# V rows of every second head from pair 12 on loaded from ScalarE's queue, with a new order of the work

## The chip, the cores and the metric

The kernel runs on one core of one Trainium2 chip. Its time is the device time of the execution in microseconds (us), and the time of a version is the median of several runs. The engines are called as in the profile: PE (TensorE; PEld are its weight loads), ACT (ScalarE), DVE (VectorE), POOL (GpSimd) and SP (SyncE, which only issues DMAs). SP and ACT each have a hardware DMA queue, POOL a software one.

## The reference

Attention over 8 batches with 8 heads of 576 positions and 64 features, in two parts that are added, followed by a two-layer network over the 4608 tokens:

```
q_d, k_d, v_d = means over groups of 4 positions            # 144 positions
out_up    = repeat(softmax(scale * q_d k_d^T) v_d, 4)        # pooled attention
out_local = softmax(scale * q k^T where |i - j| < 4) v       # a band of 7 positions
x = (out_up + out_local) as 4608 tokens x 512 features
h = x @ w_in                                                 # 512 -> 2048
result = (h - tanh(h)) @ w_out                               # 2048 -> 512
```

## The kernel before

The work comes in 32 *pairs* of heads (pair p is batch p // 4, heads 2(p % 4) and the next) and 8 *blocks* of the network, one for each batch. Four pairs make the tokens of one block. Matmuls run in bf16.

**A pair** (`attention`, `prep_v`, `pool_v`, `pool_v4`). `load_qk` brings K and Q rows into `st` (4 slots, p % 4), `load_v` brings the V rows of each of the two heads by a DMA of its own into `vst` (5 slots, p % 5; L390, 160 KB, 640 rows of 256 bytes). From pair 12 on, `load_v4` also brings V in groups of four positions (`v4`), which POOL adds up (L440, L444); the first 12 pairs pool V by matmuls (L458). Casts to bf16 follow (`qr` L502, `vw` L427), then transposes of K and Q: on PE for the first 12 pairs (L510), by DMA from SP afterwards (L556). Scores are matmuls over 64 rows (L657, L665, L671), followed on ACT by three exps (L676, L680, L684), by a mask product (L711) on DVE or POOL, by the matmuls with V (L725), by the division (L740, L742) and the way back into token columns `xT` (L767 on PE or L780 by DMA, L760).

**A block** (`dense`). 16 groups of four matmuls of 512 columns against `w_in` (L803), each followed by a tanh on ACT (L814) and a subtraction on DVE (L817, `gT`); and the second layer (L883, for the last three blocks L1030), whose results are copied out and stored. The 64 tokens of a batch beyond 512 are done for two batches at once (L829, L855). The groups of both layers take four PSUM banks in turn (`DENSE`). `w_in` and `w_out` come by four DMAs each from POOL (`load_w`, L408 and L412), held back until a tile named by `GATE` or `OGATE` has arrived (L416).

**The order.** Everything is written down as operations for a planner (`Plan`): `op` notes an operation with the engine, a cost in ns, what it reads and writes, a priority and a time before which it isn't started (`after`). `order` puts all operations on a time line greedily: of what is ready it takes, on each engine, the one with the lowest priority number, and it frees a buffer when its readers are done. `emit` then writes the program in the order of the planned starts, so the planner decides what stands behind what on each engine's queue. Where several engines can do an operation, the string `GIVEN` names one by a letter for each choice; `REL` gives the release time of each pair's casts, `ONE` the pairs whose scores are issued together, `SOFT` the pairs whose `v4` loads come from POOL. A load (`load`) is two planned operations: the issue, on the engine that is named (500 ns on SP), and the transfer, on one planned DMA resource.

**What is not in the plan.** In the built program the DMAs of both hardware queues take eight completion semaphores in turn (DMAHW0 to DMAHW7), in the order of the program and whichever engine issues them. Each issue waits until the DMA that used its semaphore before, which is the one eight places earlier, has landed. The planner knows nothing of these waits. Each engine works its instructions off in order, so what stands behind a waiting issue waits too.

Of the kernel before, what the change touches and what calls it, by code (L numbers as in the profile page):

```python
# [14 lines left out]
class Plan:  # L15
# [17 lines left out]
    def op(self, eng, ns, fn, reads=(), writes=(), pri=0, after=0.0, slack=0.0,  # L33
           port=False, opens=None, uses=(), choice=None, rows=128, share=0.4):
        i = len(self.ops)
        deps = set()
        for key in reads:
            if key in self.last_write:
                deps.add(self.last_write[key])
        for key in writes:  # L40
            if key in self.last_write:
                deps.add(self.last_write[key])
            deps.update(self.readers.get(key, ()))
        for key in reads:
            self.readers.setdefault(key, set()).add(i)
        for key in writes:
            self.last_write[key] = i
            self.readers[key] = set()
        deps.discard(i)
        names = set(uses)  # L50
        if opens and not isinstance(opens, list):
            opens = [opens]
        for o in opens or ():
            names.add(o[0])
        for n in names:
            self.users.setdefault(n, []).append(i)
        if choice:

            letter = self.given[self.choices]
            self.choices += 1  # L60
            named = [a[:4] for a in choice if a[0][0] == letter]
            choice = named or [a for a in choice if len(a) == 4]
        alts = {a[0]: a for a in choice} if choice else {eng: (eng, ns, fn, port)}
        self.ops.append(dict(alts=alts, deps=deps, pri=pri, after=after, slack=slack,
                             opens=opens, names=names, rows=rows, share=share,
                             what=(list(writes) + [None])[0]))
        return i
# [135 lines left out]
def kernel(  # L203
# [9 lines left out]
    nc = tc.nc  # L213
    B, H, S, D = q.shape
# [5 lines left out]
    SCALE = 1.0 / float(D) ** 0.5  # L220
    N_FF = Dff // 128
    N_DC = Dm // 128
    WIDE = [c == "1" for c in "1011"]
    NBLK, NR, LEFT = B, 3, S - 512
    STEP = 112
    NT = 5
# [12 lines left out]


    KIN = [c == "1" for c in "11111111111100000000000000000000"]
    HALF = [c == "1" for c in "00001000000000000000000000000000"]

    SOFT = [c == "1" for c in "00001110011000110010001001000001"]
    VIN = [c == "1" for c in "11111111111100000000000000000000"]
    BACK = [c == "1" for c in "11111111111100000000000000000000"]
    ONE = [c == "1" for c in "00000000010000001111111111111111"]
    REL = [
# [4 lines left out]
    ]  # L253

    GIVEN = (
        "..A..D.DADA.PADDADPDD.AADD..D.DD.AA.DA.ADAA....ADAD..AA..P...AP.D..AP....DDPPPDD"
        "..D..A.A...PAAAPPPAADDD.DDDDAD.ADAD.A..PPPDDDAA...A.....DA..A.AA.PD.D..ADPDDAP.P"
        "D.PP..D.DDDDD.P..DP...DADP...P....A...D.PP..DPAAPP..P.D..AD..A..DD.PPD.PA..D.P.."
        ".PPD.P........P..PDDD.PD...AAPD....D.PPDPD.A...DPPD..A.DP.DPPP....AD..DP.D.DAP.."
        "D....DPP..DAAD..DPP.D.AA.PD.PP.PPPAAPDD..P..D..DAPP.DPP.P.P.PPAA.PPP.PPPAA.D.PPP"  # L260
        "DPDP.P..DDDD.D."
    )

    const = ctx.enter_context(tc.tile_pool(name="const", bufs=1))
# [2 lines left out]
    def fixed(name, shape, dt, n=None, pool=const):  # L267
        if n is None:
            return pool.tile(shape, dt, name=name, tag=name)
        return [pool.tile(shape, dt, name=f"{name}{i}", tag=f"{name}{i}")  # L270
                for i in range(n)]
# [12 lines left out]
    st = fixed("st", [128, 2, 2, 4 * D], FP32, NST)  # L284
# [3 lines left out]
    vst = fixed("vst", [128, 2, NT, D], FP32, NVST)  # L288
# [28 lines left out]
    P = Plan(GIVEN)  # L317
# [40 lines left out]
    def load(ns, fn, keys, cost, pri, after=0.0, eng="SP"):  # L358
        op(eng, ns, fn, writes=list(keys) + [("q", keys[0])], pri=pri, after=after)
        op("DMA", cost, None, reads=[("q", keys[0])], writes=keys, pri=pri,  # L360
           share=0.18 if keys[0][0] == "vst" else 0.35)
# [22 lines left out]
    def load_v(p):  # L384
        b, j, s = p // NP, p % NP, p % NVST
        for i in range(2):
            base = v[b, 2 * j + i]

            def issue(i=i, base=base):
                nc.sync.dma_start(out=vst[s][:, i], in_=bass.AP(  # L390
                    tensor=base.tensor, offset=base.offset,
                    ap=[[D, 128], [STEP * D, NT], [1, D]]))
            load(500, issue, [("vst", s, i)], 940, 10 * p - 3000 + 5)

    def load_v4(p):
        b, h0, s = p // NP, 2 * (p % NP), p % NV4
        vv = v[b, h0:h0 + 2].rearrange("h (g c) d -> g h (c d)", c=4)
        for i in range(2):
            load(770 if SOFT[p] else 450,
                 lambda i=i: (nc.gpsimd if SOFT[p] else nc.sync).dma_start(  # L400
                     out=v4[s][0:128 - 112 * i, :, i], in_=vv[128 * i:144 - 16 * (1 - i)]),
                 [("v4", s, i)], 1000 - 870 * i, 10 * p - 3000 + 6,
                 eng="POOL" if SOFT[p] else "SP")

# [67 lines left out]
    def attention(p):  # L472
        b, j, s = p // NP, p % NP, p % 2
        sn, w, k3 = p % NST, p % NVW, p % NKQ
        early = KIN[p]
        split = HALF[p] and not early
        pri = 10 * p
# [183 lines left out]
        def score2():  # L661
            ps = at(s2)
            for hh in range(2):
                rows = slice(64 * hh, 64 * hh + 64)
                T.matmul(ps[:, hh, 0:120], kt[s][rows, STEP * 4:STEP * 4 + 128],  # L665
                         kq[k3][rows, :, 1, G0[4]:G0[4] + NG[4]],
                         start=True, stop=True)
            for i in range(2):
                for hh in range(2):
                    rows = slice(64 * hh, 64 * hh + 64)  # L670
                    T.matmul(ps[:, hh, 120 + G * i:120 + G * i + G],  # L671
                             qkd[s][rows, 128 * i:128 * i + 128],
                             qkd[s][rows, G + GAP:2 * G + GAP], start=True, stop=True)
# [15 lines left out]
        def both_scores():  # L689
            score1()  # L690
            score2()
        if not ONE[p]:
            op("PE", 220 * cold, score1, rows=64,
# [259 lines left out]
    def token_sums(kb, which):  # L953
        g = kb % 2
        a11, a12, a21, a22 = quarters(kb)
        for n, dst, x0, x1, sub, h in ((0, S0, a21, a22, 0, 2), (2, a21, a11, a21, 1, 0),
                                       (1, a11, S0, a11, 1, 0), (3, a12, a12, a11, 1, 1)):
            if n not in which:
                continue
            parts = [(0, 1)] if WIDE[n] else [(0,), (1,)]  # L960
            for es in parts:
# [182 lines left out]
        for _ in steps:  # L1144
            pass

    GATE, OGATE = ("st", 2, 0), ("vst", 1, 1)
    SEVEN = [c == "1" for c in "00000111"]
    ORDER7 = (1, 2, 6, 7, 4, 5, 3), (1, 7, 2, 6, 5, 4, 3)
    DENSE = [(7,), (6,), (5,), (4,)]  # L1150
# [37 lines left out]
    for p in range(NP):  # L1188
        if p + 1 < NP:
            load_qk(p + 1)  # L1190
        load_v(p)
# [4 lines left out]
    def load_next():  # L1196
        if nl[0] < NPAIR:
            if nl[0] % NP == 0:
                load_rest(nl[0] // NP)
            load_qk(nl[0])  # L1200
            load_v(nl[0])
            nl[0] += 1
        if nl[0] == NP + 4:
            for f in range(4):
                load_w(moe_w_out, w_out_sb, "w_out", f, OGATE if f == 0 else None)
# [66 lines left out]
```

## Time and profile before

| what | us |
|---|---|
| median of 3 runs | 324.42 |
| the runs | 323.06 to 325.06 |
| the profiled execution | 322.44 |
| its span on the core | 320.7 |
| PE busy | 309.1 |
| DVE busy | 255.3 |
| ACT busy | 207.8 |
| POOL busy | 156.8 |

A line of the timeline gives start, duration, engine, line, operation, the tile written and the tile read, and how many were merged (x4); engines with a q are their sequencers, which issue DMAs. The rows of digits cut the span into 40 slices of 8 us and give the busy share in tenths. A line of windows gives, for each engine, busy time and instructions in that stretch, then the granted clock of PE, the mean share of the 16 DMA engines (it goes above 1 where several queues are served at once) and GB/s. The line "DMA to landing" gives the time from issue to the last byte's landing.

### The profile page before, as it was taken

To read this page: it belongs to the slowest core of one execution; us is meant where nothing else is said; L and a number is where in the kernel's file an instruction comes from. 1 tells how busy PE (TensorE), PEld (TensorE's weight loads), DVE (VectorE), ACT (ScalarE), POOL (GpSimd) and SP (SyncE) were. 2 spreads that over 40 slices of the span, in tenths; PEclk is the share of its full clock that TensorE was granted. 3 is DMA by queue.
4 is the path that set the end of the run, shared out by engine and by line. 5 is a ranking of instruction groups with operands and counts; after the bars stand their busy time and mean duration, and the time that the engine had idled before them with its cause. 6 is when DMAs were issued, how large, how long until landed. Compare 5 with 4: busy or idle time off the path is not lost.

```text
span 320.7 us, 7553 instructions
## 1 busy us (share of the span) xinstructions
PE 309.1 (96%) x2831; PEld 181.0 (56%) x2831; DVE 255.3 (80%) x451; ACT 207.8 (65%) x372; POOL 156.8 (49%) x185
## 2 busy tenths in 40 slices
PE   7978999999999999999999999999899999999994
PEld 3654546554754545454655444545476667666783
DVE  5685997597888898679888999899999797656853
ACT  5884995588856776369745878579766852455210
POOL 7822664326267473537464735357794653511000
PEclk9999999999999999999999999999999999999999
DMA  8999999999999999999999999995452143200414
GB/s 218 275 219 227 279 185 247 289 277 304 240 232 274 236 210 246 224 255 195 245 222 177 269 237 251 232 223 112 94 92 57 35 49 93 67 0 3 130 36 131
DMA packets 117205, 59.23 MB, mean 185 GB/s; under 512 B 85008, under 2 KB 112592, under 8 KB 117168
## 3 DMA queue, kind: packets, MB, share of 16 engines
q1 hardware_dynamic: 111584, 52.17, 71.3%
q0 software_dynamic: 4896, 5.97, 10.0%
q10 hardware_dynamic: 688, 0.61, 0.6%
q8 instruction: 22, 0.36, 0.4%
q14 instruction: 15, 0.12, 0.1%
HBM read 43.65 MB, written 9.44 MB: 166 GB/s over the span
## 4 chain that ended last, share of the span: by engine, by line
PE 88%; DMA 7%; DVE 1%; SPq 1%; ACT 0%; POOL 0%; ACTq 0%; issue 0%; POOLq 0%
PE ps L803 34%; PE ps L883 22%; PE ps L1030 11%; DMA vst<-in_v_dram 6%; PE ps L725 5%; PE ps L829 5%; PE ps L855 4%; PE ps L657 3%; DMA sr<-in_q_dram 1%; PE ps L671 1%; PE ps L510 1%; PE ps L458 1%; PE ps L767 1%; PE ps L665 1%; SPq L366 1%; DVE xT L760 1%
## 5 line engine op out<-in xcount | busy, mean ns | idle before, releaser
L803 PE MATMUL ps<-xT,w_in_sb 128*128 128x512 bf16 x512 | 124.6, 379 | 0.0
L817 DVE TENSOR_TENSOR gT<-ps,u 128x512 bf16<-128x512 f32 x128 | 86.0, 684 | 21.2 <-ACT u L814 19.6
L814 ACT ACTIVATE u<-ps 128x512 f32<-128x512 f32 x128 | 76.1, 599 | 36.2 <-PE ps L803 33.6
L883 PE MATMUL ps<-w_out_sb,gT 128*128 128x512 bf16 x320 | 78.6, 379 | 0.0
L803 PEld LDWEIGHTS <-w_in_sb 128*128 128x128 bf16 x512 | 47.1, 98 | 47.3 <-issue 0.4
L883 PEld LDWEIGHTS <-gT 128*128 128x128 bf16 x320 | 29.2, 98 | 31.2
L444 POOL TENSOR_TENSOR vp<-v 128x256 bf16<-128x256 f32 x20 | 14.6, 730 | 58.7 <-PE ps L725 48.1
L676 ACT ACTIVATE E<-ps 128x912 bf16<-128x912 f32 x32 | 29.8, 931 | 17.8 <-PE ps L665 14.6
L1030 PEld LDWEIGHTS <-gT 128*128 128x128 bf16 x288 | 27.9, 98 | 7.5
L742 DVE TENSOR_TENSOR ln<-ps,r 128x768 bf16<-128x768 f32 x32 | 30.6, 956 | 0.9
L711 DVE TENSOR_TENSOR E<-E,mask 128x1152 bf16<-128x1152 bf16 x29 | 25.6, 882 | 4.4 <-ACT E L680 4.2
L502 POOL CAST qr<-st 128x512 bf16<-128x512 f32 x32 | 22.5, 713 | 9.3 <-DMA st<-in_q_dram 6.0
L440 POOL TENSOR_TENSOR v<-v 128x512 f32<-128x512 f32 x20 | 25.4, 1271 | 1.1
L725 PEld LDWEIGHTS <-E 128*128 128x128 bf16 x576 | 21.7, 97 | 6.1
L684 ACT ACTIVATE E<-ps 128x576 bf16<-128x576 f32 x32 | 20.9, 654 | 0.0
L583 ACT COPY kt<-kq 128x576 bf16<-128x576 bf16 x16 | 18.9, 1180 | 2.9 <-DVE kq L578 2.7
L593 POOL TENSOR_TENSOR half<-kq 128x576 f32<-128x576 bf16 x13 | 18.1, 1389 | 3.6 <-DVE kq L578 1.5
L725 PE MATMUL ps<-vw,E 128*128 128x65 bf16 x320 | 18.9, 193 | 0.0
L760 DVE TENSOR_TENSOR xT<-lT 128x336 bf16<-128x336 bf16 (+1 forms) x30 | 18.4, 655 | 0.0
L1030 PE MATMUL ps<-Tw,gT 128*128 128x256 bf16 x144 | 18.3, 273 | 0.0
L725 PE MATMUL ps<-vp,E 128*128 128x65 bf16 x256 | 18.1, 193 | 0.0
L1030 PE MATMUL ps<-w_out_sb,gT 128*128 128x256 bf16 x144 | 17.8, 273 | 0.0
(118 smaller groups left out, 434.9 us busy)
## 6 DMA issues: line engine op xcount, KB each, us to landing
vst<-in_v_dram SPq DMA_DIRECT2D x64, 160.0 KB, 4.8
st<-in_k_dram SPq DMA_DIRECT2D x32, 256.0 KB, 4.6
st<-in_q_dram SPq DMA_DIRECT2D x32, 256.0 KB, 4.6
v<-in_v_dram SPq DMA_DIRECT2D x14, 256.0 KB, 3.6
w_in_sb<-in_moe_w_in_dram POOLq DMA_DIRECT2D x4, 512.0 KB, 12.7
w_out_sb<-in_moe_w_out_dram POOLq DMA_DIRECT2D x4, 512.0 KB, 12.2
out_dram<-y SPq DMA_DIRECT2D x7, 256.0 KB, 3.8
out_dram<-y SPq DMA_DIRECT2D x7, 224.0 KB, 3.1
```

Of the source, the lines that this page charges most:

```text
L440: eng.tensor_tensor(out=v2, in0=v4[s][:, :, :, 0:128], in1=v4[s][:, :, :, 128:256], op=ALU.add)
L502: (eng, ns, lambda dst=dst, src=src, fn=fn: fn(out=dst, in_=src), port)
L676: A.activation(out=E[s][:, :, E0:E0 + 456], in_=at(s1)[:, :, PS0:512], func=AF.Exp, scale=SCALE)
L711: eng.tensor_tensor(out=el, in0=el, in1=mask.unsqueeze(1).to_broadcast([128, 2, S]), op=ALU.mult)
L725: T.matmul(po[:, hh, 65 * n:65 * n + 65], E[s][:, hh, e:e + 128], vv, start=start, stop=stop)
L742: op("DVE", 960, lambda: V.tensor_tensor(out=ln[s].rearrange("p n (h d) -> p h n d", d=D), in0=blocks()[:, :, :, 0:64], in1=r[s].unsqueeze ...
L760: eng.tensor_tensor(out=dst, in0=src, in1=add, op=ALU.add)
L803: T.matmul(at(name)[:, 0, :], w_in_sb[:, dc, fc * 128:(fc + 1) * 128], xT[dc][:, c0:c0 + 512], start=(dc == 0), stop=(dc == N_DC - 1))
L814: op("ACT", 600, lambda: A.activation(out=u[us], in_=at(name)[:, 0, :], func=AF.Tanh), reads=[("hd", kb, fc)], writes=[("u", us)], pri=-1, ...
L817: op("DVE", 690, lambda: V.tensor_tensor(out=gT[g][:, fc, :], in0=at(name)[:, 0, :], in1=u[us], op=ALU.subtract), reads=[("hd", kb, fc), ( ...
L883: T.matmul(at(name)[:, 0, :], gT[g][:, fc, ts * 128:ts * 128 + 128], w_out_sb[:, fc, :], start=(fc == 0), stop=(fc == N_FF - 1))
L1030: T.matmul(dst, left[:, f, 128 * j:128 * j + 128], right[:, f, :], start=(first and e == 0 and f == 0 and (j == 0 or apart)), stop=(e == 1 ...
```

## The change

From pair 12 on the V rows of the second head of each pair are issued by ACT instead of SP: 20 of the 64 `vst` loads. The planner gets this as an operation of ACT, with 700 instead of 940 ns for the transfer. All tables that steer the order are new (`REL`, `GIVEN`, `SOFT`, `ONE`), and with them the order on every engine. `HALF` and `SOFT` do nothing for the first 12 pairs. `GATE` lets `w_in` start when Q of pair 2 has arrived, not K. `WIDE` cuts one of the sums over `gT` of the last three blocks (L965) into halves.

```diff
-    WIDE = [c == "1" for c in "1011"]
+    WIDE = [c == "1" for c in "1001"]
...
-    HALF = [c == "1" for c in "00001000000000000000000000000000"]
+    HALF = [c == "1" for c in "00001101100000000000000000000000"]
+    VACT = [c == "1" for c in "00000000000011111111111111111111"]
-    SOFT = [c == "1" for c in "00001110011000110010001001000001"]
+    SOFT = [c == "1" for c in "00000101010000110100000000000010"]
...
-    ONE = [c == "1" for c in "00000000010000001111111111111111"]
+    ONE = [c == "1" for c in "00000000001001001111111110111110"]
     REL = [
-           0, 0, 0, 0, 4, 14, 33.5, 30,
-           23, 49, 67, 11.5, 75, 4.5, 95, 64,
-           110, 71, 18, 23.5, 139, 151, 139.5, 148,
-           170.5, 170.5, 15, 153.5, 207.5, 209.5, 232.5, 235,
+           0, 0, 0, 0, 22.5, 12.5, 35, 16.5,
+           43.5, 51, 14.5, 46, 75.5, 39.5, 10.5, 92.5,
+           98.5, 117.5, 94, 134, 142, 150, 86.5, 130,
+           144, 86, 193, 193.5, 218, 230, 128.5, 151,
     ]
...
             def issue(i=i, base=base):
-                nc.sync.dma_start(out=vst[s][:, i], in_=bass.AP(
-                    tensor=base.tensor, offset=base.offset,
-                    ap=[[D, 128], [STEP * D, NT], [1, D]]))
-            load(500, issue, [("vst", s, i)], 940, 10 * p - 3000 + 5)
+                (nc.scalar if VACT[p] and i else nc.sync).dma_start(
+                    out=vst[s][:, i], in_=bass.AP(
+                        tensor=base.tensor, offset=base.offset,
+                        ap=[[D, 128], [STEP * D, NT], [1, D]]))
+            load(500, issue, [("vst", s, i)], 700 if VACT[p] and i else 940,
+                 10 * p - 3000 + 5, eng="ACT" if VACT[p] and i else "SP")
...
-    GATE, OGATE = ("st", 2, 0), ("vst", 1, 1)
+    GATE, OGATE = ("st", 2, 1), ("vst", 1, 1)
```

The built program shows how the instructions move. Where the counts change:

| instructions | before | after |
|---|---|---|
| `vst` loads on SP / on ACT | 64 / 0 | 44 / 20 |
| `v4` loads on SP / on POOL | 28 / 12 | 32 / 8 |
| casts to `qr` on POOL / DVE / ACT | 32 / 20 / 12 | 39 / 18 / 7 |
| casts to `vw` on POOL / DVE / ACT | 11 / 6 / 15 | 13 / 5 / 14 |
| `kt` from `kq` (L583, L584) on ACT / DVE | 16 / 4 | 12 / 8 |
| sums L965 on DVE, whole / half; on POOL | 5 / 0; 1 | 3 / 6; 0 |
| matmuls that only fill holes (L1240) | 19 | 18 |
| runs of 64-row score matmuls on PE | 44 | 42 |

On ACT's queue the first of the moved loads (pair 12, slot 2 of `vst`) stands behind the tanh of group 12 of block 0 and the cast of pair 7's V, which frees the slot, and ahead of the tanhs of groups 13 to 15. It takes semaphore DMAHW6, which K of pair 8 on SP has used before it. On SP four loads of pooled V (`v4` of pairs 12 and 13) now stand ahead of V and K of pair 8; before, all four stood behind K of pair 8, two of them also behind its Q.

More of the change, by code (lines that the diff above doesn't have):

```diff
@@ L241 @@
     KIN = [c == "1" for c in "11111111111100000000000000000000"]
-    HALF = [c == "1" for c in "00001000000000000000000000000000"]
-    SOFT = [c == "1" for c in "00001110011000110010001001000001"]
+    HALF = [c == "1" for c in "00001101100000000000000000000000"]
+    VACT = [c == "1" for c in "00000000000011111111111111111111"]
+    SOFT = [c == "1" for c in "00000101010000110100000000000010"]
     VIN = [c == "1" for c in "11111111111100000000000000000000"]
     BACK = [c == "1" for c in "11111111111100000000000000000000"]
-    ONE = [c == "1" for c in "00000000010000001111111111111111"]
+    ONE = [c == "1" for c in "00000000001001001111111110111110"]
     REL = [
[4 rows of a table removed]
[4 rows of a table added]
     ]
     GIVEN = (
[L256 to L261, printed above, removed]
+        "P.AP.D.A...DDD.AAA.DAP.A.DA....A.AP.A.DD.DA.PAP.....DD.D...A.AP...........DPP..."
+        ".PDPD.DAP.PD.AP..AD.DAPDPPAD.....A.D.....P.AADPPDADAP..P.DPP.D.AA.PP.AA..P....P."
+        "DAP....D..PD..P.P..PAP.A.D..P...PPA.D.............DD.PDA..DPDA.P.D....D..DD...PP"
+        "P.....P.PPP.D.PA.P.D.P.D.ADA.DDDDDDDP.PPPDADP.DD.PA..DADDD.PPAD.P.APPDP..D..A.PP"
+        ".D..D....PDA..DD.PPDDPADDP.P....P.....D.PP.DD...DDP.AAD.....A..AA.D.DP.PD.D..D.P"
+        "P...DDD.DD.D...DDD"
     )
```

## The prediction

> **What bounds the kernel now.** I read the page first (busy times, slices, the chain that ended last), then busy time by windows, then the timelines of SP and of ACT between 38 and 60 us, and last each DMA's time to landing.
>
> ```profile
> PE 309.1 (96%) x2831; PEld 181.0 (56%) x2831; DVE 255.3 (80%) x451; ACT 207.8 (65%) x372; POOL 156.8 (49%) x185
> ...
> PE   7978999999999999999999999999899999999994
> ...
> DMA  8999999999999999999999999995452143200414
> ...
> PE 88%; DMA 7%; DVE 1%; SPq 1%; ACT 0%; POOL 0%; ACTq 0%; issue 0%; POOLq 0%
> ```
>
> TensorE is the bound. From 30.4 us on its matmuls follow each other without a hole until 316.5, but for 1.1 us before 231.9 (L829 waits for DVE). The DMA row shows the second full resource: transfers fill the 16 engines until 215 us, in the first 60 us above all:
>
> ```profile
> 13.00:33.00 20.00, 16.46 (x255) 11.39 (x253) 14.63 (x35) 14.52 (x32) 7.56 (x11) 1.00 1.20 234
> ...
> 38.00:58.00 20.00, 20.00 (x194) 10.86 (x192) 15.39 (x31) 15.51 (x31) 11.71 (x15) 1.00 1.16 227
> ```
>
> In these two windows the weights arrive (L408, L412, on POOL's queue) beside the loads of SP. PE is full in the second (20.00 of 20.00): the late loads cost it nothing, since it works on pairs that arrived before. How late they are, SP's timeline tells:
>
> ```profile
> 41.58 0.59 SPq L366 DMA_DIRECT2D st<-in_k_dram  x1
> 42.22 1.14 SPq L400 DMA_DIRECT2D v<-in_v_dram  x2
> 43.45 0.37 SPq L366 DMA_DIRECT2D st<-in_q_dram  x1
> 44.20 5.25 SPq L400 DMA_DIRECT2D v<-in_v_dram  x2
> 50.16 3.88 SPq L390 DMA_DIRECT2D vst<-in_v_dram  x2
> 54.13 1.32 SPq L366 DMA_DIRECT2D st<-in_k_dram  x1
> 55.71 1.81 SPq L366 DMA_DIRECT2D st<-in_q_dram  x1
> 57.61 1.27 SPq L390 DMA_DIRECT2D vst<-in_v_dram  x2
> ```
>
> These are K of pair 8, pooled V of 12, Q of 8, pooled V of 13, V of 9, K and Q of 9, V of 10. For the first, and then the third, the source view says:
>
> ```profile
> DMA to landing us min/median/max: 12.1/12.1/12.1
> DMA to landing us min/median/max: 14.4/14.4/14.4
> ```
>
> So K of pair 8 lands at 41.58 + 12.1 = 53.7 and Q at 57.9. Each issue waits for the landing of the hardware DMA eight places earlier in the program (the eight semaphores used in turn): Q of pair 9 is issued at 55.71, and eight places ahead stands the pooled V of 42.22, landed 13.4 later, at 55.65. Set beside the matmul that stands just ahead of it in the program, V of pair 10 (57.61) belongs to a matmul that ran at 40.9: SP runs 16.7 us behind its place. From 90 us to 215 it is 0 to 5 us behind.
>
> **The change part by part.** The sum is against the profiled execution: 322.44 us, a span of 320.7 and 1.7 around it, which is 2.0 below the median of the runs, 324.42.
>
> *Twenty V loads move from SP to ACT.* SP loses 20 issues of about 0.55 us (4.78 for four at 76.96 are more, 0.94 for two at 159 less): 11 us on a queue that sets no end. ACT gains 20 of about 0.65 (the two `sr` issues on ACT took 0.67 and 0.64): 13 us on 207.8. Without waits this lies in ACT's 113 us of idle time; where ACT is fullest (8.85 of 10 us from 80) one issue delays a tanh by 0.65, and PE has four PSUM banks of 0.86 us each ahead of it. I take 0, bounds 0 to 2.
>
> *The first of them, for pair 12, brings a wait.* In the changed program's ACT order it stands between the tanh of `h` 12 of block 0, with the cast of pair 7's V, and the tanh of `h` 13; it uses semaphore DMAHW6, whose last user is K of pair 8, on SP. ACT gets there at about 43.3: tanh 12 can start at 42.0 (tanh 12 in the trace before: 42.46), 0.60, then the cast, 0.73. K of pair 8 lands at 53.7 if it comes as before. But four loads of pooled V (576 KB) now stand ahead of it on SP, and sharing with `w_out` lasts to 57.9; by bytes it then takes the place of Q of pair 8, 57.9. POOL sends `w_in` about 1.5 us earlier (the mask product of 2.36 us ahead of its gate is gone; the gate now waits for Q of pair 2, which landed at 11.6, where it ran at 13.16), so both may come 0 to 1.5 earlier. Bounds 52.2 to 57.9; I take 57.0, near the upper one, since order on the queue decides.
>
> Behind the issue on ACT wait: tanh 13, 14 and 15 of block 0 (0.60 each), exp 2 and 3 of pair 5 (0.36, 0.65). Who waits for these: on DVE `gT` 13 to 15 and the mask of pair 5 (0.9 to 1.4), then PE's `out` of pair 5 (L725). PE's order ahead of that one: MM1 of block 0 to its end, 10 matmuls L883 at 0.216 and 8 transposes at 0.056. The useful PE work before the first L883 adds up to 29.2 us in both programs (counts times pace: 0.216 for 512 columns, 0.056 for 128, 0.031 for 65); that matmul ran at 46.15, so PE stops at 46.15 + 2.16 + 0.45 = 48.8. It resumes after the issue (0.65), three tanh (1.80), exp 2 (0.36), the mask (1.2) and about 0.7 of signals and `gT` 15: 4.7 after the landing, at 61.7. PE is stopped for 12.9 us (52.2: 8.1; 57.9: 13.8). Nothing covers this: afterwards 266.7 us of matmuls remain, back to back in both orders.
>
> *PE restarts after rest.* The nearest row: the first seven L1240 took 3.11 us, where seven of the same size took 1.67 at 221.64. The only other hole, 1.4 us before 30.38, was followed by full pace (eight in 1.89). A stop of 12.9 is nearer to the first: +1.4, bounds 0 and 1.4. The Trainium skill ("TensorE: Matmul & The Clock Gate", Part 1: The HAM clock gate) says that an idle window of about 3.4 us halves the clock and that some 3.4 us of work restore it; by it the term would be 1.7, an estimate. The trace's granted clock reads 1.00 throughout, so no row here shows the gate itself.
>
> *The other 19 issues.* I took every hardware DMA of the program before and set the landing of the one eight places earlier against the matmul at its place: between 40 and 60 us it landed 15 us after that matmul (median), between 60 and 80, 7.2, between 80 and 215, from 3.8 before it to 2.0 after it, but for three at 80 to 82 (up to 3.4). Issues 2 to 5 fall in the second stretch, but once PE is 12.9 late that lag is used up (V of pair 11, which issue 2 waits for, landed at 65.8; ACT now gets there at about 68). The rest have at most 2 us, mostly under PE's banks: +0.5, bounds 0 and 6.
>
> *The new order.* Matmuls: one filler less, 512 + 320 + 288 as before. Runs of 64-row score matmuls fall from 44 to 42; each switch shows as 0.15 after and 0.10 before the run: -0.5. The hole at 231.9 may go or come back: -0.5, bounds -1.1 and +1. The start: w_out's first part landed at 45.17, the first L883 ran at 46.15, so at most 1.0 is to be had there, and the stop at 48.8 eats it: 0. SOFT moves two pooled loads from POOL to SP (4 x about 0.5 us, SP's lag); the WIDE sums are split after 235 us on DVE (6 halves for 3 wholes of 1.3 us, one of which POOL had: 1.3 us of DVE's 20% idle time): 0. Casts moved between engines: 0 beside the stop.
>
> Sum: 322.4 + 12.9 + 1.4 + 0.5 - 0.5 - 0.5 = 336.2 on the profiled scale; with 2.0 to the median, 338.
>
> **The rivals.**
> 1. *No wait to speak of, 323.* Issue 1 finds DMAHW6 free. It needs K of pair 8 landed by 48.8 - 4.7 = 44.1. For it: SP has fewer issues, and PE never waited for such data before. Against: at 44.1 before, K was 2.5 us past its issue, with V of pair 8 still in flight (49.1). Then 322.4 - 1.0 + 2.0 = 323.4.
> 2. *Faster, 320.* As 1, and the start gains: `w_out` 1.5 us earlier, first L883 up to 2.5 earlier, the hole gone, two switches: 324.4 - 2.5 - 1.1 - 0.5 = 320.3. It decides only if issue 1 passes before 44.1. The Trainium skill ("DMA: Bandwidth & Descriptors", Issuing engines are not separate DMA queues) speaks against it: issuing from a second engine saves only the sequencer's time. The trace agrees as far as it goes (share 1.16 with two queues busy).
> 3. *More waits, 343.* Attention of pairs 6 and 7 starts late, issues 2 to 5 wait again, POOL's and DVE's queues need time to refill: 3 to 8 us more than the sum.
> 4. *A short stop, 328.* The issue waits, but the backlog is smaller (landing near 48): PE loses 3 to 6.
>
> **How the numbers follow.** A difference of 1% is about what a measurement of this kernel can tell from none. Forecast with its bounds, 331 to 342: 0.64; rival 3: 0.12; rival 4, 326 to 331: 0.08; rival 1: 0.12; rival 2: 0.04. Leaving out rivals 1 and 2 and the top of 3 gives 326 to 345. Slower by over 1% (above 327.7): 0.64 + 0.12 + 0.05 = 0.81; within 1%: 0.12 + 0.03 = 0.15; faster: 0.04.
>
> **What would show it.** Right: an ACT hole of 10 us or more that starts near 43 us and ends with the issue for pair 12; PE idle from about 49 to 62, before an L725; SP's K of pair 8 landing at 52 to 58; seven slow matmuls after the hole; from 80 us on waits under 2 us; matmuls from 62 to the end lasting some 267. Wrong: the issue for pair 12 taking under 1 us from ACT's last instruction, or PE's digits at 9 through the whole middle: then SP was not behind.

## The result, and the profile after

The changed kernel takes 339.51 us (median of 4 runs, 339.33 to 340.27), the kernel before, on the same chip, 324.17 (4 runs). The ratio is 1.048, with a 95% interval of 1.044 to 1.052. 338.0 was forecast, with a range of 326 to 345. The profiled execution took 339.62 us, with a span of 337.7 on the core; set beside the profiled 322.44 of before, 17.2 us more. In the changed file the lines named so far lie 2 to 4 further down (`vst` loads L392, pooled V L404, transposes L514, exps L680 to L688, `out` L729, w_in matmuls L807, tanh L818, `gT` L821, w_out matmuls L887, fillers L1244).

The page of the changed kernel, lines of its parts 1, 2 and 4:

```profile
PE 308.7 (91%) x2786; PEld 182.5 (54%) x2830; DVE 253.1 (75%) x450; ACT 202.9 (60%) x369; POOL 157.8 (47%) x188
...
PE   7978950599999999999999999999999999999995
...
DVE  5868710546896878988897998899887978775853
ACT  4967800456878488676875647768757773264310
POOL 7622810243684859565745555576690760002000
PEclk9999985599999999999999999999999999999999
DMA  8999899956938999999999995997362602300324
...
PE 80%; DMA 11%; SPq 4%; ACT 2%; issue 1%; POOL 1%; ACTq 0%; DVE 0%; POOLq 0%
```

One slice of PE is empty and its neighbours are half full (slices 5 to 7, counted from 0, 42 to 68 us); from slice 8 on the row is as full as before. ACT's row is empty in slices 5 and 6, and DVE's and POOL's rows nearly so. No engine has much more work than before (POOL 157.8 us against 156.8): the time is lost to waiting. PE's share of the chain fell from 88% to 80%, and DMA and SP's sequencer took the difference. The row PEclk says that the granted clock fell in slices 5 to 7; in the row of before it never falls. By windows:

```profile
38.00:58.00 20.00, 8.80 (x57) 3.94 (x56) 4.89 (x9) 3.98 (x8) 5.81 (x9) 0.73 1.10 209
58.00:80.00 22.00, 17.07 (x168) 10.37 (x171) 11.66 (x24) 10.60 (x24) 8.36 (x10) 0.78 0.80 198
80.00:215.00 135.00, 133.60 (x1155) 71.13 (x1174) 114.75 (x197) 95.76 (x170) 83.03 (x93) 1.00 1.01 223
```

From 38 to 80 us PE works 25.87 (8.80 + 17.07) of 42 us, where it worked all of the time before: 16.1 us of idle time lie there, beside a low clock (0.73, 0.78) while it works. From 80 us on it is full again at 1.00 (133.60 of 135; 44 of the 2830 matmuls have no record in this trace). Of ACT's timeline between 40 and 62 us:

```profile
41.55 0.72 ACT L431 CAST vw<-vst 128x640 bf16<-128x640 f32 x1
59.76 0.48 ACTq L392 DMA_DIRECT2D vst<-in_v_dram  x1
60.34 1.57 ACT L818 ACTIVATE u<-ps 128x512 f32<-128x512 f32 x3 [18.06 <-DMA st<-in_k_dram]
61.79 0.39 ACT L684 ACTIVATE E<-ps 128x240 bf16<-128x240 f32 x1
62.04 0.68 ACT L688 ACTIVATE E<-ps 128x576 bf16<-128x576 f32 x1
```

After the cast of pair 7's V, which ends at 42.27, ACT stands for 17.5 us in front of one issue (ACTq), the first of the moved loads. The bracket names what ended it: a K load, not the V that ACT wanted to issue. Behind it come the three tanhs and the two exps of pair 5 that the prediction listed. SP's timeline and the source view of that K load (pair 8) tell when it landed: 49.14 + 10.5, which is 59.68 in the trace's finer times, 0.08 ahead of the issue:

```profile
43.91 4.34 SPq L380 DMA_DIRECT2D sr<-in_k_dram  x1
48.29 0.75 SPq L380 DMA_DIRECT2D sr<-in_q_dram  x1
49.14 0.54 SPq L368 DMA_DIRECT2D st<-in_k_dram  x1
```

```profile
DMA to landing us min/median/max: 10.5/10.5/10.5
```

And PE's timeline:

```profile
44.41 0.81 PE L1244 MATMUL ps<-lT 128*128 128x512 bf16 x3
47.39 0.58 PE L887 MATMUL ps<-w_out_sb,gT 128*128 128x512 bf16 x1 [2.18 <-DMA w_out_sb<-in_moe_w_out_dram]
48.20 1.06 PE L887 MATMUL ps<-w_out_sb,gT 128*128 128x512 bf16 x2 [0.22 <-issue]
62.77 0.58 PE L514 MATMUL ps<-ident,qr 128*128 128x128 bf16 x4 [13.52 <-ACT E L688]
63.15 0.63 PE L538 MATMUL ps<-ident,rr 128*128 128x128 bf16 x4
63.58 2.76 PE L887 MATMUL ps<-w_out_sb,gT 128*128 128x512 bf16 x6
...
67.76 1.48 PE L887 MATMUL ps<-w_out_sb,gT 128*128 128x512 bf16 x6
```

Three things stand in it. PE waits 2.18 us for the first part of w_out (landed at 47.35; before, at 45.17). It stops for 13.52 us ahead of the transposes of pair 7's Q, which need the PSUM bank that exp 3 of pair 5 reads. And after the stop six L887 take 2.76 us, where six take 1.48 at 67.76. The first two are one loss of 15.7 us: between them PE runs only the four L887 that stand ahead of the transposes in its order (one has no record), and the stretch ends when ACT's exp 3 does. With w_out in time PE would have come to the same place earlier and waited there longer.

### The profile page after: what moved, and what is told of

It is laid out like the page before. It is cut to its first block, busy times and chain, and to the rows that moved or that the text cites. A ratio compares the mean times of both kernels' runs of the same rounds, so it can differ in the third digit from the quotient of the medians.

```text
span 337.7 us, 7516 instructions
## 1 busy us (share of the span) xinstructions
PE 308.7 (91%) x2786; PEld 182.5 (54%) x2830; DVE 253.1 (75%) x450; ACT 202.9 (60%) x369; POOL 157.8 (47%) x188
## 4 chain that ended last, share of the span: by engine, by line
PE 80%; DMA 11%; SPq 4%; ACT 2%; issue 1%; POOL 1%; ACTq 0%; DVE 0%; POOLq 0%
PE ps L807 29%; PE ps L887 21%; PE ps L1034 11%; DMA vst<-in_v_dram 6%; PE ps L729 5%; PE ps L833 4%; PE ps L859 4%; DMA st<-in_k_dram 3%; PE ps L661 3%; DMA sr<-in_q_dram 2%; SPq L380 1%; SPq L392 1%; SPq L368 1%; PE ps L675 1%; PE ps L514 1%
## 5 line engine op out<-in xcount | busy, mean ns | idle before, releaser
L807 PE MATMUL ps<-xT,w_in_sb 128*128 128x512 bf16 x487 | 122.5, 379 | 1.4 <-issue 0.5
L821 DVE TENSOR_TENSOR gT<-ps,u 128x512 bf16<-128x512 f32 x128 | 86.5, 685 | 40.0 <-ACT u L818 38.9
L818 ACT ACTIVATE u<-ps 128x512 f32<-128x512 f32 x128 | 76.1, 600 | 59.7 <-PE ps L807 38.0
L887 PE MATMUL ps<-w_out_sb,gT 128*128 128x512 bf16 x305 | 80.3, 387 | 3.2 <-DMA w_out_sb<-in_moe_w_out_dram 2.2
L807 PEld LDWEIGHTS <-w_in_sb 128*128 128x128 bf16 x512 | 47.5, 98 | 49.7 <-DMA w_in_sb<-in_moe_w_in_dram 2.0
L887 PEld LDWEIGHTS <-gT 128*128 128x128 bf16 x320 | 29.3, 99 | 33.0 <-issue 4.3
L680 ACT ACTIVATE E<-ps 128x912 bf16<-128x912 f32 x32 | 29.9, 935 | 15.1 <-PE ps L669 7.8
L448 POOL TENSOR_TENSOR vp<-v 128x256 bf16<-128x256 f32 x20 | 15.9, 794 | 48.9 <-PE ps L729 38.7
L506 POOL CAST qr<-st 128x512 bf16<-128x512 f32 x39 | 27.3, 711 | 7.7 <-PE ps L514 4.8
L715 DVE TENSOR_TENSOR E<-E,mask 128x1152 bf16<-128x1152 bf16 x29 | 23.3, 805 | 4.7 <-ACT E L684 4.5
L729 PEld LDWEIGHTS <-E 128*128 128x128 bf16 x576 | 22.3, 98 | 7.0 <-issue 0.6
L514 PE MATMUL ps<-ident,qr 128*128 128x128 bf16 x96 | 9.4, 229 | 14.1 <-ACT E L688 13.5
L602 POOL TENSOR_TENSOR qkd<-half 128x288 bf16<-128x288 f32 x19 | 16.2, 855 | 10.4 <-DVE half L597 6.2
L688 ACT ACTIVATE E<-ps 128x576 bf16<-128x576 f32 x32 | 21.0, 657 | 0.0
L1105 POOL TENSOR_TENSOR y<-y,keep 128x512 f32<-128x512 f32 x4 | 6.2, 1561 | 30.4 <-ACT y L1055 30.4
L729 PE MATMUL ps<-vw,E 128*128 128x65 bf16 x320 | 19.3, 194 | 0.1
L729 PE MATMUL ps<-vp,E 128*128 128x65 bf16 x256 | 18.3, 195 | 0.0
L597 POOL TENSOR_TENSOR half<-kq 128x576 f32<-128x576 bf16 x10 | 15.0, 1497 | 6.9 <-DVE kq L582 5.0
```

The source lines that it names most:

```text
L506: (eng, ns, lambda dst=dst, src=src, fn=fn: fn(out=dst, in_=src), port)
L680: A.activation(out=E[s][:, :, E0:E0 + 456], in_=at(s1)[:, :, PS0:512], func=AF.Exp, scale=SCALE)
L688: A.activation(out=E[s][:, :, EP:EW].rearrange("p h (i c) -> p h i c", i=2)[:, :, :, 0:G], in_=at(s2)[:, :, 120:408].rearrange("p h (i c) ...
L715: eng.tensor_tensor(out=el, in0=el, in1=mask.unsqueeze(1).to_broadcast([128, 2, S]), op=ALU.mult)
L729: T.matmul(po[:, hh, 65 * n:65 * n + 65], E[s][:, hh, e:e + 128], vv, start=start, stop=stop)
L807: T.matmul(at(name)[:, 0, :], w_in_sb[:, dc, fc * 128:(fc + 1) * 128], xT[dc][:, c0:c0 + 512], start=(dc == 0), stop=(dc == N_DC - 1))
```

## The experiments

The theory: an issue on ACT's queue waits for the landing of the hardware DMA eight places earlier; SP's loads land some ten us late between 40 and 70 us, so the wait is long there, and PE needs what stands behind it on ACT. The rivals: the new order costs the time (A); the 20 issues cost ACT's time (B); PE would have waited for late data anyway (C). All in one table, ratios to the kernel before on the same chip:

| run | what differs | us | ratio, 95% interval |
|---|---|---|---|
| changed | | 339.51 | 1.048, 1.044 to 1.052 |
| e1 | all V loads on SP, new order | 325.67 | 1.005, 1.001 to 1.008 |
| e2 | pair 12 on SP, 19 on ACT | 334.18 | 1.029, 1.025 to 1.033 |
| e3 | pair 12 on ACT, 19 on SP | 340.07 | 1.047, 1.042 to 1.052 |
| e4 | half of w_out's bytes | 333.28 | 1.026, 1.023 to 1.029 |
| e5 | pairs 12 to 16 on SP, 15 on ACT | 326.03 | 1.006, 1.003 to 1.009 |
| e6 | 125 fillers in the stop | 339.16 | 1.046, 1.040 to 1.051 |
| e7 | old order, 20 loads on ACT | 342.40 | 1.059, 1.053 to 1.064 |
| e8 | e5, planned anew with pooled V later | 341.00 | 1.051, 1.045 to 1.057 |
| e9 | e5, pooled V behind pair 8 on SP | 327.55 | 1.012, 1.008 to 1.016 |
| e10 | 100 fillers in the stop | 339.27 | 1.048, 1.042 to 1.053 |
| e11 | kernel before, 15 loads from ACT | 334.48 | 1.031, 1.025 to 1.036 |
| e12 | pairs 12 to 16 from POOL's queue | 325.36 | 1.004, 1.001 to 1.007 |

### Which issue carries it: e1, e2, e3

Each changes only the engine named in `issue`; the plan and every other engine's order stay as in the changed kernel.

```diff
-                (nc.scalar if VACT[p] and i else nc.sync).dma_start(
+                nc.sync.dma_start(                                        # e1
+                (nc.scalar if p > 12 and i else nc.sync).dma_start(       # e2
+                (nc.scalar if p == 12 and i else nc.sync).dma_start(      # e3
```

> The new order as it is, but SP issues all 64 V loads at the same places of the program. Theory (the first issue on ACT waits for K of pair 8): ACT has no hole from 42 to 60 us; the stop of 13.5 us before L514 and the slow restart after it (3.1 us) are gone, so the profiled execution comes from 339.6 to about 323, within 2 of the kernel before (324). The wait of 2.2 us for w_out before the first L887 may stay. Rival A, the new order itself is worse (four loads of pooled V ahead of pair 8 make K of pair 8 late for TensorE as well): it stays above 330. Rival B, the 20 issues take ACT's time: it falls by some 13 us of ACT work, but spread over the span, with no single hole to go.

> Only the first moved load (pair 12) goes back to SP; 19 stay on ACT. Theory: the wait passes to the second one (pair 13), which takes the semaphore of V of pair 11: without the first stop ACT comes to it at about 56 us (72.3 less the 16.5 that are gone), and that load lands at about 67. So a hole of some 11 us on ACT from 56 to 67, a stop of TensorE of 7 to 10 us near 60, and 330 to 335 in all. Rival: the first issue alone is special (it stands ahead of tanhs and exps that TensorE needs at once), later ones are covered: 322 to 326, like all on SP.

> Only the first moved load (pair 12) stays on ACT; the other 19 go back to SP. Theory: that one issue carries the whole loss, the other 19 at most 0.5 us: 338 to 340, with the same hole on ACT from 42 to 60. Rival (20 issues on ACT, each 0.65 us, share the loss): about a twentieth of the loss of 15.4, 324 to 326.

All three came out as the theory has it. e1 takes 325.67, so the new order by itself costs 0.5% (rival A falls). Its PE row has no empty slice; the 6 in slice 5 is the wait for w_out (2.70 us). So PE does not wait for other late data either (rival C falls):

```profile
PE   6979969999999999999999999999999999999994
```

e3, with a single load on ACT, takes as long as with twenty (340.07; rival B falls). In e2 the stop passes to the second issue. ACT's timeline of e2:

```profile
56.56 0.66 ACT L688 ACTIVATE E<-ps 128x576 bf16<-128x576 f32 x1
68.62 0.43 ACTq L392 DMA_DIRECT2D vst<-in_v_dram  x1
69.15 0.38 ACT L467 CAST vp<-ps 128x256 bf16<-128x256 f32 x1 [11.94 <-DMA vst<-in_v_dram]
```

and PE's:

```profile
70.28 0.61 PE L514 MATMUL ps<-ident,qr 128*128 128x128 bf16 x4 [7.12 <-ACT qr L506]
```

ACT reaches the issue for pair 13 at 57.2 and stands until 68.62; V of pair 11, eight places earlier, was issued at 63.70 and landed 4.9 later, at 68.56. ACT's hole (11.94) and PE's stop (7.12) are those expected.

### How long the wait is: e4

```diff
+        V.memset(w_out_sb[:, :, 256:512], 0.0)
...
-                GP.dma_start(out=dst[:, 4 * f:4 * f + 4, :],
+                GP.dma_start(out=dst[:, 4 * f:4 * f + 4, 0:256],
...
-                             [:, 4 * f:4 * f + 4, :])
+                             [:, 4 * f:4 * f + 4, 0:256])
```

> As the changed kernel, all orders and semaphores the same, but only columns 0 to 255 of w_out are loaded (the other half of w_out_sb is zero, one memset on DVE at the start), so the four w_out transfers bring 2.1 MB less. Theory: at about 230 GB/s that is 9.1 us less ahead of K of pair 8, which lands near 50.5 instead of 59.7; ACT's hole ends with it, TensorE resumes near 53.7 instead of 62.8, restart up to 3 us better: 327 to 331. Rival (the stop is set by something else than that landing, such as the number of loads on SP's queue or the exps themselves): 337 to 340, for the w_out wait alone 2 less.

SP's, ACT's and PE's timelines of e4 (its lines are one further down):

```profile
44.44 0.54 SPq L369 DMA_DIRECT2D st<-in_k_dram  x1
```

```profile
54.01 0.49 ACTq L393 DMA_DIRECT2D vst<-in_v_dram  x1
54.60 1.57 ACT L819 ACTIVATE u<-ps 128x512 f32<-128x512 f32 x3 [11.97 <-DMA st<-in_k_dram]
```

```profile
46.41 1.02 PE L888 MATMUL ps<-w_out_sb,gT 128*128 128x512 bf16 x4 [0.84 <-DMA w_out_sb<-in_moe_w_out_dram]
57.03 0.58 PE L515 MATMUL ps<-ident,qr 128*128 128x128 bf16 x4 [9.60 <-ACT E L689]
```

K of pair 8 lands at 53.94, 5.74 earlier than in the changed kernel; the issue follows 5.75 earlier, PE resumes 5.74 earlier, and the whole takes 6.2 less (333.28; the profiled executions differ by 5.74). No order was changed, only the bytes on another queue, and one memset at the start was added: the stop's end follows that landing one for one. The wait for w_out fell as well, from 2.18 to 0.84 us, and gave nothing on top of the 5.74: beside the stop it costs nothing. The size was expected too large (9.1 us, 2.1 MB at 230 GB/s): the last part of w_out landed only 5.7 earlier (52.29 against 57.98).

### Whether the semaphore is what it waits for: e12

```diff
-                (nc.scalar if VACT[p] and i else nc.sync).dma_start(
+                (nc.sync if not VACT[p] or not i else nc.scalar if p > 16
+                 else nc.gpsimd).dma_start(
```

> The changed kernel with the second heads of pairs 12 to 16 issued by POOL, at the same places of the program, on its software queue, whose DMAs take semaphores of their own; pairs 17 to 31 stay with ACT. Theory: the wait comes from the semaphores that SP's and ACT's queues share, so on POOL's queue the issue for pair 12 waits for no landing of SP's loads, and TensorE does not stop for it: 324 to 329 (five issues of 0.8 us on POOL and what they delay there). Rival (V of pair 12 needs something else that comes late, such as its slot or room in the DMA rings): POOL stands at the issue until near 59, and TensorE with it: 330 to 340.

POOL's timeline of e12:

```profile
42.22 0.62 POOL L506 CAST qr<-st 128x512 bf16<-128x512 f32 x1
43.09 0.90 POOL L392 DMA_DIRECT2D vst<-in_v_dram  x1 [0.25 <-ACT vw L431]
44.01 0.81 POOL L602 TENSOR_TENSOR qkd<-half 128x288 bf16<-128x288 f32 x1
```

The same load, at the same place of the program, with the transfers just as crowded (K of pair 8 lands at 61.06, later than in the changed kernel): POOL issues it 0.25 us after the cast that frees its slot, 16.7 us earlier than ACT, and the time is 325.36. So neither the slot nor late data (rival C) is the cause. What is left is the semaphore: in the built program ACT's issue for pair 12 waits for DMAHW6 and for the cast that frees the slot, and for nothing else. In eight profiles the first issue on ACT that waits starts 0.06 to 0.10 us after the landing of the DMA eight places earlier, whichever that is (in e6, e8, e10 and e12 it does too, 0.07 to 0.10 us after it):

| run | issue for pair | eight places earlier | landed | issued |
|---|---|---|---|---|
| changed | 12 | K of 8 | 59.68 | 59.76 |
| e2 | 13 | V of 11 | 68.56 | 68.62 |
| e3 | 12 | K of 8 | 59.29 | 59.36 |
| e4 | 12 | K of 8 | 53.94 | 54.01 |
| e5 | 17 | Q of 15 | 86.46 | 86.55 |
| e7 | 12 | pooled V of 13 | 58.52 | 58.62 |
| e9 | 17 | Q of 15 | 85.46 | 85.56 |
| e11 | 17 | K of 15 | 82.10 | 82.19 |

### Whether it needs the new order, and where the move is free: e7, e5, e11

e7 gives the kernel before, with its own tables, only the queue (in `load_v`, with the plan's operation on ACT, so the planner places the 20 issues itself). e5 and e11 leave pairs 12 to 16 with SP, in the new order and in the old one; every other engine's order is unchanged.

```diff
+                (nc.scalar if p > 11 and i else nc.sync).dma_start(       # e7
+                (nc.scalar if p > 16 and i else nc.sync).dma_start(       # e5, e11
```

> The kernel before with all its own tables, and only the 20 V loads planned and issued on ACT. Theory: the new order is not needed for the loss. The planner puts the issue for pair 12 again ahead of three tanhs and of exp 2 and 3 of pair 5; its semaphore was used last by the second pooled V of pair 13, which landed at 58.95 in the kernel before. ACT comes to it at about 43 to 45, so a hole of some 14 us, a stop of TensorE of 10 to 13 and its restart: 336 to 341. Rival (the new tables put the issue where it hurts): 323 to 328.

> The new order; the second heads of pairs 12 to 16 stay with SP, those of pairs 17 to 31 (15 loads) go from ACT. Theory: only the issues that ACT reaches while SP's loads land ten us after their turn cost something; from pair 17 on (near 83 us) the load eight places earlier has landed or is within 2 us of it. So it equals all on SP: 324 to 327, no ACT wait for a DMA above 3 us behind an issue. Rival (each issue on ACT costs its own 0.65 us in the full part of the kernel): 15 x 0.65 = 10 more, 333 to 336.

> The kernel before, its order and its plan kept on every engine; only the engine that issues 15 loads is another: the second heads of pairs 17 to 31 go from ACT. Theory: where no landing is awaited, the move neither gains nor costs: SP is not what TensorE waits for, and each issue on ACT takes 0.65 us with work beside it: 323.5 to 325.5. Rival (loads on a second queue arrive earlier or faster and help): below 322. Rival (ACT is too full after 80 us): above 327.

ACT's and PE's timelines of e7:

```profile
59.15 1.57 ACT L816 ACTIVATE u<-ps 128x512 f32<-128x512 f32 x3 [15.18 <-DMA v<-in_v_dram]
```

```profile
60.52 2.72 PE L885 MATMUL ps<-w_out_sb,gT 128*128 128x512 bf16 x6 [13.44 <-DVE gT L819]
```

The old order does it as well: an ACT hole of 15.18 us from 44.0, a stop of 13.44 that ends at 60.52, and 342.40 in all, 1.4 above what was expected. e5 gave the time expected, but not quite for the reason: ACT waits 3.2 us for Q of pair 15, and PE 2.35. e11 refutes "from pair 17 on it is free": 334.48, 10 more than before. ACT's and PE's timelines of e11:

```profile
77.81 0.60 ACT L814 ACTIVATE u<-ps 128x512 f32<-128x512 f32 x1 [0.61 <-PE ps L803]
82.19 0.41 ACTq L390 DMA_DIRECT2D vst<-in_v_dram  x1
82.65 0.93 ACT L676 ACTIVATE E<-ps 128x912 bf16<-128x912 f32 x1 [4.24 <-DMA st<-in_k_dram]
```

```profile
83.63 0.56 PE L657 MATMUL ps<-kq,kt 64*128 64x112 bf16 x8 [3.53 <-ACT E L676]
84.13 1.89 PE L803 MATMUL ps<-xT,w_in_sb 128*128 128x512 bf16 x4
```

It is the same wait once more. Where an exp that PE needs stands right behind the issue, 3.8 us of wait (78.41 to 82.19) are 3.5 us of stop, and the low clock after it adds to that (four L803 in 1.89 us, where five took 1.24 at 78.86). The issue for pair 29, at 189.94, likewise waits for Q of pair 27, landed at 189.88: a hole of 3.1 us on ACT, 1.3 on PE. In the profiled execution, which is 9.6 us above the profiled one of before, another 2.8 us are lost by 58 us, ahead of any moved issue on ACT (last section).

### The slow restart: e6, e10

```diff
+            if o["what"] == ("tqd", 7):
+                self.fill(125)          # e10: 100
...
+    def fill(n):
+        for _ in range(n):
+            T.matmul(bank[:, 1, 256:512], warm[:, 0:128], warm[:, 0:256],
+                     start=True, stop=True)
```

> The changed kernel with 125 matmuls of 256 columns (results unused, in the free upper half of a PSUM bank) put into TensorE's order just ahead of the transposes before which it stops. At 0.108 us each they last 13.5 us, from 49.3 to 62.8, when the stop ends. Theory (after the stop the clock is low for some 4 us, which is the 3.1 us that the following matmuls take too long): the clock reads 1.00 at 62 to 68, the six L887 after it go at full pace, and the time falls by 2.5 to 3.1, to 336.4 to 337.0. Rival (the slow restart is a wait for other engines that come back late with TensorE): no gain, 339 to 340.

> The changed kernel with 100 fillers instead of 125. With 125 they kept TensorE until 64.7, 1.9 us longer than the stop had lasted, which can have hidden the gain. 100 of them end near 61.5 to 62, before the stop does. Theory (the clock, low after rest, costs 2.3 to 3.1 us): 336.3 to 337.3, with the six L887 after the stop at 1.46 us instead of 2.76. Rival (the slow restart is no matter of the clock's): 339 to 340.

The windows view with PE alone (busy time, granted clock, DMA share, GB/s), first of the changed kernel, then of e6:

```profile
46.00:48.00 2.00, 0.58 (x1) 0.84 1.15 235
...
50.00:62.00 12.00, 0.00 (x0) 0.50 1.19 238
...
64.00:66.00 2.00, 2.00 (x6) 0.50 1.21 295
66.00:68.00 2.00, 2.00 (x29) 0.54 1.13 233
68.00:70.00 2.00, 2.00 (x22) 1.00 1.02 306
```

```profile
50.00:62.00 12.00, 12.00 (x103) 0.92 1.15 245
...
64.00:66.00 2.00, 2.00 (x21) 1.00 1.16 313
66.00:68.00 2.00, 2.00 (x32) 1.00 1.07 216
```

With fillers the clock is back before the stop ends and reads 1.00 after it, and the six L887 take 1.46 us instead of 2.76. But the median did not fall, since 125 fillers took 14.58 us (the first ones at the low clock that the wait for w_out had left, hence 0.92) and held PE until 64.68, 1.9 later than the changed kernel resumes. (One of e6's four runs, not the profiled one, took 336.32.) From PE's resumption to the end of the span e6 takes 337.3 - 64.68 = 272.6 us, the changed kernel 337.7 - 62.77 = 274.9, and in neither does PE wait again: the low clock costs 2.3. In e10 100 fillers ended 4.43 us too early, since w_out came earlier there and they ran at the full clock throughout; the clock fell to 0.50 once more, PE resumed 0.65 later than in the changed kernel, and the time is 339.27, as the rival had it, though not for its reason. So the rows show that the slow restart is the clock's, and what it costs is the difference of two stretches of the profile. Neither run's median shows the gain, since neither run's fillers ended with the stop.

### The first part of w_out: e8, e9

```diff
+                 after=50000.0 if p in (12, 13) else 0.0,                  # e8, load_v4
...
+        v = [i for i in order if self.engine[i] == "SP"
+             and self.ops[i]["what"][0] == "v4"][:4]                        # e9, emit
+        to = [i for i in order if self.engine[i] == "SP"
+              and self.ops[i]["what"] == ("st", 0, 1)][2]
+        order = [i for i in order if i not in v]
+        x = order.index(to) + 1
+        order = order[:x] + v + order[x:]
```

> As the run with pairs 12 to 16 left to SP, but the pooled V of pairs 12 and 13 (four loads, 0.58 MB) is not issued before 50 us in the plan, so that it no longer stands beside the first part of w_out. Theory: w_out's first part lands near 45.2 again, as in the kernel before, instead of 47.4 to 48.2; the wait of 1.6 to 2.7 us before the first L887 shrinks to under 1 and the clock stays up after it: 321.5 to 324.5. Rival (w_out is late because POOL's queue or w_in comes later): 325 to 327, no change.

> As the run with pairs 12 to 16 left to SP, all orders the same but for one edit on SP's queue: the four pooled V loads of pairs 12 and 13 stand behind K and Q of pair 8 again, as most of them did in the kernel before. (In the earlier try the whole plan was made anew, and stops after 80 us hid the answer.) Theory: w_out's first part lands near 46.8 instead of 48.3 and K of pair 8 near 55.5 instead of 59.4; the wait ahead of the first L887 falls from 3.07 to about 1.5: 1 to 1.5 us less than that run, 324.5 to 325.2. Rival (those loads do not matter to w_out): the same as that run, 326.

e8 tells little: a release time makes the whole plan anew, and 341.00 comes from stops elsewhere, among them 2.7 us that end at 84.6, behind an issue on ACT, and 3.2 that end at 299.9, before matmuls that wait for `xT`. e9 moves just four issues on SP. w_out's first part lands at 46.37 (e5: 48.28) and the wait ahead of L887 falls from 3.07 to 0.78, so those loads do set it: in the eight profiles with the loads ahead of pair 8 and all of w_out it lands at 47.0 to 48.6, in the five without (before, e7, e8, e9, e11) at 45.2 to 46.8.

The time did not follow: 327.55, where 324.5 to 325.2 was expected and e5 has 326.03. PE, earlier now, loses a part again behind the issue for pair 17: it waits 3.16 us until 88.7 where e5 waits 2.35 until 89.8, since the landing that the issue waits for is only 1.0 us earlier. And in e9 the granted clock was 0.91 from 20 to 40 us, where e5 has 1.00, ahead of all that the edit moves. The profiled execution of e9 is the shorter of the two (326.58 against 327.46). What the edit is worth in time stays open.

No version beat the kernel before. The best of the changed ones are e12 and e1, 0.4 and 0.5% behind it.

## Why the prediction was right

By its own steps, all on the profiled scale:

- *The wait.* Right, issue, semaphore and predecessor: K of pair 8 was to land at 57.0 (bounds 52.2 to 57.9) and landed at 59.68. The upper bound was too low: it let the K load take the place of Q in the old queue, by bytes, but with four more loads ahead SP also came later to it (one `sr` issue took 4.34 us), and K was issued at 49.14, not at 41.58. With those loads behind pair 8 again (e9) it is issued at 42.20 and lands at 57.49, inside the bounds. The reason given for the upper end, that the order on the queue decides, is the smaller part: e9's K is issued 4.7 us earlier than e5's and lands 1.9 earlier, while half of w_out's bytes bring the landing 5.74 forward (e4).
- *The stop.* Right in kind, mis-sized: 12.9 forecast, 15.7 of idle time measured (2.18 + 13.52). PE was to stop at 48.8 ahead of `out` (L725) and to resume 4.7 after the landing; it stopped ahead of the transposes of pair 7's Q, and resumed 3.1 after it. The error: the list of who waits for exp 3 named the mask and `out`, but not the PSUM bank that exp 3 frees. So six w_out matmuls and eight transposes (1.30 + 0.45 us), which were counted as done ahead of the stop, came after it. Landing 2.7 late, tail 1.6 shorter, stop 1.75 of work earlier: 12.9 + 2.7 - 1.6 + 1.75 = 15.75. The second of these hid a part of the others.
- *The start.* Costed at 0, since what it gives the stop eats. It did not gain but lost: w_out's first part came 2.2 later, by the four pooled loads that had been counted on SP's queue but not against the transfers of POOL's (e9), and PE waited 2.18 for it. The 0 holds all the same, for the reason given: the stop ends with exp 3 on ACT, whatever PE did before, and in e4 a wait shorter by 1.34 gave nothing on top of the landing. Without the stop the wait counts in full: e1 has 2.70, and a low clock after it.
- *The restart.* 1.4 forecast (the rule of the Trainium skill cited there would have made it 1.7), 2.3 measured by e6 against the changed kernel. The row chosen, seven matmuls at the start, was the right kind of row, but too short a stretch: the granted clock stays at 0.50 for about 5 us after the stop. The prediction had said that no row of before shows the gate; the profile after shows the fall and the return.
- *The other 19 issues.* 0.5 forecast; e3, without them, takes 0.6 more than with them, within the noise. But this holds since PE was already late by some 16 us: without the first stop the second issue leaves a hole of 11.9 us on ACT (e2), and without the first five the sixth waits 3.2 to 4.2 (e5, e11, e9). The remark that the lag is used up once PE is late was the right reason.
- *The order.* -1.0 forecast for the hole at 231.9 and the switches. The hole (0.97 in the trace) went, in the changed kernel and in e1. Yet e1 as a whole is 0.5% above the kernel before, the wait for w_out and the low clock after it having taken more than the hole gave.

The three terms close the account, as an estimate: PE resumes at 62.77 with four w_out matmuls done, which the kernel before has at 47.0 (46.15 + 4 x 0.216), so it is 15.8 behind; 2.3 for the restart and 1.0 less for the hole make 17.1, and the profiled executions differ by 17.2.

Rival 3 (more waits) did not come true: PE waits for nothing more after 62.77, and issues 2 to 20 cost nothing that shows (e3). Rivals 1 and 2 needed K of pair 8 landed by 44.1, and it landed at 59.68. The sum came to 336.2 on the profiled scale where 339.6 was measured, 3.4 under. That 338 lies within 1.5 of the median is in part luck: 2.0 was added since the profiled execution of before lay 2.0 below its median, and that of the changed kernel lies 0.1 above its own.

## What to carry to other kernels

Before a DMA goes to another engine's queue, find which semaphore its issue will wait for and when the DMA that used it last lands, and then what stands behind the issue on that engine: SP, which only issues, stood up to 16.7 us behind in the kernel before while PE stayed full; ACT, which also computes, hands its wait on to what stands behind the issue. A load that is early by the plan is not early where the queues are 10 us behind; to judge such a move, set every issue's place in its engine's order against landings from a trace, and do so again for the second issue once the first one's wait is gone. When a stop is costed, list also the PSUM banks that the delayed instructions free, and the low clock after it.

## What the runs showed of the hardware

- *The clock after short stops.* The granted clock fell to 0.50 in the stops of 7.1 to 13.9 us, and came back 3.6 (e3) to 5.1 us (changed kernel) after PE resumed; in e10, after a stop of 4.43, it came back after 2.6. It also fell around waits of 1.89 us (e12: 0.91 from 46 to 48, 0.50 from 48 to 50), of 2.18 (changed kernel: 0.84 from 46 to 48) and of 2.70 (e1, where six L887 at 49.6 took 2.77), but not after one of 3.07 in e5 or of 1.4 in the kernel before. The Trainium skill ("TensorE: Matmul & The Clock Gate", Part 1: The HAM clock gate) says that the clock drops after an idle window of about 3.4 us and rises after as much work. The half clock and, roughly, the time to come back agree; the wait of 3.07 without a fall does not speak against it, the falls around waits of 1.89 to 2.70 do.
- *POOL's issue did not wait.* e12's issue on POOL passed at once where ACT's stood for 17.5 us. The Trainium skill ("DMA: Bandwidth & Descriptors", Why a DMA increments its semaphore by 16 and not by 1) says that two DMAs in flight on one semaphore can let a wait pass too early, and asks for one semaphore for each slot in flight. That would be a reason for an issue to wait for the semaphore's last user; no run here tries it without. That the issue does wait here, the table of landings shows.
- *One order, two sets of landings.* In e11 nothing differs from the kernel before until 82 us, but w_out was issued at 37.94 instead of 38.20, a little ahead of pair 8's V instead of level with it. The second half of that V landed at 52.49 instead of 49.10, K of pair 8 at 57.12 instead of 53.66, and PE was 2.8 us late by 58 (the L510 that ran at 55.10 ran at 57.91). That the 0.3 us are the cause is not shown. Why the two executions fell out differently, and whether all six runs of e11 did so, stays open.
